# One core, attention with a SoLU layer: the order in which each engine's operations go out is taken from a table

## Chip, core and metric

The kernel runs on one NeuronCore of a Trainium2 chip. The metric is the time of the device in microseconds, the median of the runs shown. Engines are called by the profile's short names: PE (TensorE's matmuls), PEld (its weight loads), DVE (VectorE), ACT (ScalarE), POOL (GpSimd), SP (SyncE, which only issues DMAs here).

## What is computed

```python
def _attn_ref(q, k, v):             # 4 batches, 8 heads, 1152 positions, 64 wide
    q_pool = q.reshape(B, H, S // 2, 2, D).mean(axis=3)
    scores = scale * np.matmul(q_pool, k.transpose(0, 1, 3, 2))
    scores = scores - np.max(scores, axis=-1, keepdims=True)
    attn = np.exp(scores)
    attn = attn / (np.sum(attn, axis=-1, keepdims=True) + 1e-09)
    return np.matmul(attn, v)

def _moe_ref(x, w_in, w_out, g_ln):  # 2304 tokens, 512 -> 1024 -> 512
    h = x @ w_in
    e = np.exp(h - h.max(-1))
    solu = h * e / (e.sum(-1) + 1e-9)
    ln = (solu - mean) / np.sqrt(var + 1e-06) * g_ln
    return ln @ w_out
```

The output of the attention, heads side by side, is the x of the second part.

## The kernel before

The work is 32 heads (16 pairs), each with 9 blocks of 128 keys, and 18 tiles of 128 tokens. Nearly all products run as sums of f16 parts (a high and a low part of each operand), which is why every tensor is split before it is used.

For a pair P, `pair` (from line 614) loads K, Q and V, scales and splits them (tiles kn, qn on ACT and DVE), transposes the parts by DMA on SP (`k_turn`, `q_turn2`) and copies halves of them to other partitions (`k_stack`, `q_low`, `q_twice`, `q_half`). For a head g, `maxima` (from line 934) multiplies Q and K once to find the row maxima (PE at line 450 through the helper `mm`, DVE reductions mx at line 959), turns them into a row of shifts c5 and has SP write it into the operand q2 (`put`, lines 977 to 982). `scores` (from line 1092) then runs over the 9 key blocks j: two products of 288 columns each with the shift built in, Exp on ACT into e and eh (lines 1127 and 1133), the low part on POOL or DVE (line 1150), the products with V in PSUM bank 7 (`values`), and a division into the tile x.

When all 8 heads of a batch are done, `tokens` (from line 1286) takes their four or five tiles of tokens: split (xn), transposed by DMA (xt, line 1306), product with w_in into two banks, maxima, Exp, the product e (line 1338), the normalization (line 1375) with two small steps on POOL before it, the split into ln, its transpose (lt, ltt, line 1388), product with w_out, copy and store (lines 1441 and 1446). For the last batch nothing of attention is left beside this.

Nothing is issued straight away. Each step calls `Plan.add` (line 82) with an engine, a length in ns, a due time, a function that issues it, and the keys that it reads and writes. OFF (line 22) shifts the due time by key. `Plan.run` (line 110) plays a list scheduling: in simulated time each engine takes the ready operation with the earliest due time, with fixed costs for signals between engines, PSUM banks and rotating buffers. Where nothing is ready in the head it puts in a filler on PE (a transpose at line 1542). For SP the simulated end is that of the DMA:

```python
busy[e] = t + 640 * o.calls
dma = max(dma, t + 1200) + length
o.end = dma + KP.get("DL", 1000)
```

KP sets DL to 2000, and `TRD, TRC = KP["TR"]` are 300 and 2. At the end the functions are called in the order of their simulated starts (lines 284 to 286). That order is each engine's queue on the chip, and every engine works its queue off in order. Waits between engines are put in by the framework, from what is read and written.

Of the kernel before, what the change touches and what calls it, by code (L numbers as in the profile page):

```python
# [1573 lines left out]
```

## Time and profile before

| | us |
|---|---|
| median of 3 runs | 662.02 (661.11 to 669.67) |
| the profiled execution | 661.14 |
| its span | 659.4 |
| granted clock, mean | 0.986 |

A row of a timeline gives start, duration and what ran; in brackets stands how long the engine had been idle and what released it. Busy times of PE contain modelled ends, so neighbouring matmuls overlap in it. A granted clock of 1.00 is 2.4 GHz, of 0.50 it is 1.2 GHz.

### The profile page before, as it was taken

To read this page: it belongs to the slowest core of one execution; us is meant where nothing else is said; L and a number is where in the kernel's file an instruction comes from. 1 tells how busy PE (TensorE), PEld (TensorE's weight loads), DVE (VectorE), ACT (ScalarE), POOL (GpSimd) and SP (SyncE) were. 2 spreads that over 40 slices of the span, in tenths; PEclk is the share of its full clock that TensorE was granted. 3 is DMA by queue.
4 is the path that set the end of the run, shared out by engine and by line. 5 is a ranking of instruction groups with operands and counts; after the bars stand their busy time and mean duration, and the time that the engine had idled before them with its cause. 6 is when DMAs were issued, how large, how long until landed. Compare 5 with 4: busy or idle time off the path is not lost.

```text
span 659.4 us, 17549 instructions
## 1 busy us (share of the span) xinstructions
PE 607.0 (92%) x6821; PEld 422.1 (64%) x6821; DVE 493.6 (75%) x980; ACT 522.0 (79%) x1231; POOL 445.8 (68%) x376
## 2 busy tenths in 40 slices
PE   8986989899879899998999999998899999989996
PEld 7864877687556656675676666665566666654442
DVE  5997799889996977968697968696878875545450
ACT  4793778879898878988898989897889898864361
POOL 4692665559669877688878787867968689841140
PEclk9997999999999989999999999999999999999999
DMA  9786748694947667565758573939395642035444
GB/s 232 164 206 137 159 130 192 154 207 87 159 90 128 132 117 161 111 141 127 151 92 172 129 149 72 202 83 179 76 173 110 104 89 58 19 73 113 91 76 89
DMA packets 201903, 84.65 MB, mean 128 GB/s; under 512 B 189020, under 2 KB 189020, under 8 KB 201820
## 3 DMA queue, kind: packets, MB, share of 16 engines
q1 hardware_dynamic: 201820, 83.54, 60.9%
q8 instruction: 53, 0.87, 0.6%
q14 instruction: 30, 0.25, 0.1%
HBM read 36.70 MB, written 4.72 MB: 63 GB/s over the span
## 4 chain that ended last, share of the span: by engine, by line
PE 56%; DVE 17%; ACT 14%; DMA 5%; issue 4%; POOL 2%; SPq 1%; DVEq 0%; ACTq 0%; POOLq 0%
PE bank L450 53%; DVE mx L959 6%; ACT e L1127 3%; ACT eh L1127 3%; DMA xt<-xn 2%; PE bank L1542 2%; DVE kn L456 2%; DMA raw<-in_moe_w_out_dram 1%; DVE e L1375 1%; POOL eh L1150 1%; ACT e L1331 1%; DVE e L1338 1%; DVE qn L456 1%; ACT kn L715 1%; ACT vlo L847 1%
## 5 line engine op out<-in xcount | busy, mean ns | idle before, releaser
L1150 POOL TENSOR_TENSOR eh<-e,eh 128x576 f16<-128x576 f32 x255 | 337.3, 1333 | 115.7 <-ACT e L1127 35.4
L959 DVE TENSOR_REDUCE mx<-bank 128x2 f32<-128x768 f32 (+1 forms) x264 | 202.8, 785 | 48.2 <-PE bank L450 47.7
L1127 ACT ACTIVATE eh<-bank 128x288 f16<-128x288 f32 x384 | 151.5, 428 | 37.5 <-PE bank L450 36.0
L1127 ACT ACTIVATE e<-bank 128x288 f32<-128x288 f32 x426 | 166.5, 432 | 13.4 <-PE bank L450 7.8
L450 PE MATMUL bank<-q,w 128*128 128x288 f16 (+1 forms) x576 | 161.0, 291 | 8.7 <-ACT e L1127 3.5
L450 PE MATMUL bank<-q,w2h 65*128 65x288 f16 x540 | 150.2, 290 | 0.0
L450 PEld LDWEIGHTS <-eh 128*128 128x128 f16 x3855 | 138.2, 98 | 18.0 <-issue 2.3
L450 PE MATMUL bank<-vhi,eh 128*128 128x65 f16 x2570 | 143.1, 194 | 2.1 <-POOL eh L1150 1.1
L450 PE MATMUL bank<-vlo,eh 128*128 128x64 f16 x1285 | 133.4, 193 | 0.0
L450 PE MATMUL bank<-w,q 128*128 128x384 f16 (+1 forms) x390 | 101.7, 333 | 15.2 <-DVE mx L959 14.3
L450 PE MATMUL bank<-wb,lt 128*128 128x512 f16 x360 | 96.9, 381 | 7.3 <-DVE e L1338 5.7
L450 PE MATMUL bank<-wb,xt 128*128 128x512 f16 x360 | 98.0, 378 | 2.7 <-DMA xt<-xn 2.7
L450 PEld LDWEIGHTS <-w2h 65*128 65x128 f16 x540 | 53.1, 98 | 39.3 <-issue 12.0
L450 PEld LDWEIGHTS <-w 128*128 128x128 f16 x540 | 53.9, 100 | 30.3 <-issue 3.1
L450 PEld LDWEIGHTS <-lt 128*128 128x128 f16 x360 | 35.1, 98 | 34.2 <-issue 7.2
L450 PEld LDWEIGHTS <-q 128*128 128x128 f16 x360 | 33.5, 100 | 36.0 <-issue 21.0
L1133 ACT ACTIVATE eh<-bank 128x576 f32<-128x576 f32 (+1 forms) x75 | 46.8, 652 | 11.0 <-PE bank L450 10.7
L450 PEld LDWEIGHTS <-xt 128*128 128x128 f16 x360 | 34.1, 97 | 28.9 <-DMA xt<-xn 4.0
L1319 DVE TENSOR_REDUCE st<-bank 128x1 f32<-128x512 f32 x36 | 24.6, 684 | 28.7 <-PE bank L450 28.7
L450 PE MATMUL bank<-vx,eh 128*128 128x65 f32 x310 | 39.8, 276 | 0.0
L450 PEld LDWEIGHTS bank<-vx,eh 128*128 128x128 f32 x310 | 38.7, 196 | 0.9 <-issue 0.2
L1369 POOL TENSOR_SCALAR st<-st 128x1 f32<-128x1 f32 x18 | 5.1, 284 | 40.7 <-ACT ln L1360 40.0
(138 smaller groups left out, 833.5 us busy)
## 6 DMA issues: line engine op xcount, KB each, us to landing
kt<-in_k_dram SPq DMA_DIRECT2D x32, 288.0 KB
qt<-in_q_dram SPq DMA_DIRECT2D x16, 576.0 KB
vx<-in_v_dram SPq DMA_DIRECT2D x32, 288.0 KB
out_dram<-o SPq DMA_DIRECT2D x36, 128.0 KB
q<-q SPq DMA_DIRECT2D x30, 144.0 KB
w2h<-w SPq DMA_DIRECT2D x30, 144.0 KB
khi<-w SPq DMA_DIRECT2D x30, 144.0 KB
raw<-in_moe_w_in_dram SPq DMA_DIRECT2D x8, 511.6 KB
```

The costliest lines, as they stand in the source:

```text
L450: nc.tensor.matmul(out=o, lhsT=a, rhs=b, start=first, stop=last, skip_group_check=True)
L456: eng.scalar_tensor_tensor(out=o, in0=a, scalar=scale, in1=b, op0=ALU.mult, op1=ALU.subtract)
L715: nc.scalar.activation(out=o, in_=tl["kt", P], func=ACTF.Copy, scale=tl["qs", P][:, 2:3])
L847: nc.scalar.activation(out=new(("vlo", P), [128, 2, NJ, D], F16), in_=tl["vt", P], func=ACTF.Abs, accum_out=new(("am", P), [128, 1], F32),)
L959: nc.vector.tensor_reduce(out=flat(tl["mx", g])[:, i:i + n], in_=tl[place(i, n)], op=ALU.max, axis=AXX)
L1127: nc.scalar.activation(out=tl[name, (g, j)][:, f * HALF:(f + 1) * HALF], in_=tl[tn(j, f), (g, j, f)], func=ACTF.Exp, scale=esc,)
L1133: nc.scalar.activation(out=new((name, (g, j)), [128, SQ * 4 // mybir.dt.size(dtype)], dtype)[:, 0:SQ].rearrange("p (f i) -> p f i", f=2), ...
L1150: eng.tensor_tensor(out=e[:, o:o + c.stop - c.start], in0=e32[:, c], in1=e[:, c], op=ALU.subtract)
L1319: nc.vector.tensor_reduce(out=st(f), in_=tl[H_[f]], op=ALU.max, axis=AXX)
L1331: nc.scalar.activation(out=tl[E][:, f * 512:(f + 1) * 512], in_=tl[H_[f]], func=ACTF.Exp, bias=st(2), scale=xs[:, r, 3:4], accum_out=st(3 ...
L1338: nc.vector.scalar_tensor_tensor(out=tl[E][:, s], in0=tl[H_[f]], scalar=xs[:, r, 3:4], in1=tl[E][:, s], op0=ALU.mult, op1=ALU.mult, accum_ ...
L1542: plan.warm = lambda i: nc.tensor.transpose(bank[:, i, 0:128], ident, ident)
```

## The change

OFF gets new values for its 924 keys but the one for qn.5, which is new. A table SEQ is added: for each engine a string with one letter for each operation; the letter's code less 80 is a shift. The new method `line` sorts each engine's operations by their simulated start, as before, and then puts at place i the operation that stood at place i plus the shift. It also works out what each operation needs (its dependences, the users of the buffers and banks that it takes over, the makers of earlier buffers of the same tag), and calls the functions in an order that keeps these needs and each engine's own order. A new argument `late` adds to the simulated end of transposes by DMA. The engines, the buffers, the instructions and KP are the same.

```diff
--- before.py
+++ after.py
@@ -19,7 +19,8 @@
 AXX = mybir.AxisListType.X
 
...
-OFF = {'am.0': 15.58, 'am.1': 0.67, 'am.10': -8.76,
...
+OFF = {'am.0': 13.09, 'am.1': -0.54, 'am.10': -9.87,
...
+SEQ = {'PE': 'PPPPPPPPPPPPPPPPPPPPPPPPPQOPPPPPPPPPPPPPPPPPRPQRLOPPPPPPPPPPPPPPPPPPPPPPPPPPPPPPPPPPPPPPPPPPPPPPPPPPPPPPPPPPPPPPPPPPPPUOOSNOMPPQTPPRXNIPSOOOUIQ
...
 FIRST = KP.get("L0", 0.3)
 
 
@@ -79,9 +80,9 @@
                 yield from list(self.parts[k])
             yield k
 
-    def add(self, engine, length, at, fn, reads=(), writes=(), mark=None, kind="round", also=(), calls=1):
+    def add(self, engine, length, at, fn, reads=(), writes=(), mark=None, kind="round", also=(), calls=1, late=0):
         at += OFF.get(self.group((writes or reads)[0]), 0)
-        o = Op(n=len(self.ops), engine=engine, length=length, at=at, fn=fn, mark=mark, kind=kind, calls=calls)
+        o = Op(n=len(self.ops), engine=engine, length=length, at=at, fn=fn, mark=mark, kind=kind, calls=calls, late=late)
         deps = o.deps
         for k in self._keys(reads):
             if k in self.writers:
@@ -122,7 +123,7 @@
         for o in sorted(ops, key=lambda o: o.at):
             for b in o.new:
                 order[b[0]].append(b)
-        where, before = {}, {}
+        where, before, tags_of = {}, {}, defaultdict(list)
         ready = {e: [] for e in self.HOP}
         busy = dict.fromkeys(ready, 0)
         ranks = dict.fromkeys(ready, 0)
@@ -254,6 +255,7 @@
                     self.bank[b] = c
                 else:
                     turn[self.tags[b[0]][0]] += 1
+                    tags_of[self.tags[b[0]][0]].append(o)
                 head[b[0]] += 1
             for d in (*o.deps, *(x for b in o.uses for x in before.get(b, ()))):
                 known[e][d.engine] = max(known[e][d.engine], d.rank)
@@ -267,7 +269,7 @@
             if e == "SP":
                 busy[e] = t + 640 * o.calls
                 dma = max(dma, t + 1200) + length
-                o.end = dma + KP.get("DL", 1000)
+                o.end = dma + KP.get("DL", 1000) + o.late
             else:
                 busy[e] = o.end = t + length
             if o.mark is not None:
@@ -281,9 +283,51 @@
         if done < len(ops):
             raise ValueError([(o.n, o.engine, o.at, o.uses, o.left) for o in ops if o.start is None][:30])
         self.end = max(busy.values())
-        calls = [(o.start, o.n, o.fn) for o in ops] + [(t, -1, fn) for t, fn in extra]
-        for _, _, fn in sorted(calls, key=lambda x: x[:2]):
+        for fn in self.line(extra, where, tags_of):
             fn()
+
+    def line(self, extra, where, tags_of):
+        ops = self.ops
+        self.bufedges = defaultdict(set)
+        users, maker, tenant, need = defaultdict(list), {}, {}, {o: set(o.deps) for o in ops}
+        for o in ops:
+            for b in o.uses:
+                users[b].append(o)
+        for o in sorted(ops, key=lambda o: (o.start, o.n)):
+            for b in o.new:
+                maker[b] = o
+                for i in where[b]:
+                    if i in tenant:
+                        self.bufedges[o].update(users[tenant[i]])
+                    tenant[i] = b
+        for o in ops:
+            need[o].update(self.bufedges[o])
+            need[o].update(maker[b] for b in o.uses)
+            need[o].discard(o)
+        for made in tags_of.values():
+            for x, o in zip(made, made[1:]):
+                if x is not o:
+                    need[o].add(x)
+        self.need, self.items = need, {}
+        todo = {}
+        for e in self.HOP:
+            x = [(o.start, o.n, o.fn, o) for o in ops if o.engine == e]
+            if e == "PE":
+                x += [(t, -1, fn, None) for t, fn in extra]
+            x.sort(key=lambda x: x[:2])
+            self.items[e] = x
+            todo[e] = [x[i + ord(c) - 80] for i, c in enumerate(SEQ[e])] if SEQ else x
+            assert len({id(y) for y in todo[e]}) == len(x)
+        at, done, calls = dict.fromkeys(todo, 0), set(), []
+        while len(calls) < sum(len(x) for x in todo.values()):
+            heads = [(todo[e][at[e]][:2], e) for e in todo if at[e] < len(todo[e])]
+            heads = [(k, e) for k, e in heads if k[1] < 0 or need[todo[e][at[e]][3]] <= done]
+            _, e = min(heads)
+            _, _, fn, o = todo[e][at[e]]
+            at[e] += 1
+            done.add(o)
+            calls.append(fn)
+        return calls
 
 
 def MM(n, c=1):
@@ -755,7 +799,7 @@
             add("ACT", ACT(2 * SQ, 1, 1), at, k_hi, [KT, S_], [(*KN, 0)])
             add(*(("DVE", 2 * DVE(SQ) + 500) if P >= KP["KL"] else ("POOL", 2 * POOL(SQ))), at, k_lo, [KT, S_, (*KN, 0)], [(*KN, 1)])
             for h in range(2):
-                add("SP", TRD, at + KD * h + 0.5, lambda h=h: k_turn(h), [KN], [("w1", G + h, 0)], calls=TRC)
+                add("SP", TRD, at + KD * h + 0.5, lambda h=h: k_turn(h), [KN], [("w1", G + h, 0)], calls=TRC, late=1100)
             for h in range(2):
                 add("SP", DMA(64 * S * 2, 200), at + KD * h + 0.55, lambda h=h: k_stack(h), [("w1", G + h)], [("khi", P, h)])
 
@@ -824,7 +868,7 @@
             add("DVE", DVE(SQ) + 450, at, q_lo2, [*QT_, S_, (*QN, 0)], [(*QN, 1)])
             T, T1, T2 = ([(k, P, c, h) for h in range(2)] for k, c in (("q1", "T"), ("q1", "t"), ("q2", "t")))
             for h in range(2):
-                add("SP", TRD / 2, at + 0.5 + h / 10, lambda h=h: q_turn2(h), [QN], [T[h]], calls=TRC)
+                add("SP", TRD / 2, at + 0.5 + h / 10, lambda h=h: q_turn2(h), [QN], [T[h]], calls=TRC, late=1200)
             add("SP", DMA(64 * S * 2, 200), at + 0.8, q_low, T, T2)
             add("SP", DMA(64 * S * 2, 200), at + 0.9, q_twice, [*T, *T2], T1)
             add("SP", DMA(128 * 128, 200), at + 3, q_half, [("q1", P)], [("zq", P)], calls=2)
@@ -1391,7 +1435,7 @@
         SX = ("xs", r, 1)
         add("ACT", ACT(512, 1, 1), at, x_hi, [key, SX], [(*XN, 0)])
         add("DVE", DVE(512) + 400, at, x_lo, [key, (*XN, 0), SX], [(*XN, 1)])
-        add("SP", TRD, at + 0.2, x_turn, [XN], [XT], calls=TRC)
+        add("SP", TRD, at + 0.2, x_turn, [XN], [XT], calls=TRC, late=1100)
         for f in range(2):
             for c in range(6):
                 a = at + 1 + (6 * f + c) * step
@@ -1422,7 +1466,7 @@
             add("POOL", POOL(DF) + 80, a2, lambda: l_lo(nc.gpsimd), [E, (*LN, 0)], [(*LN, 1)])
         else:
             add("DVE", DVE(DF) + (700, 100)[tail], a2, lambda: l_lo(nc.vector), [E, (*LN, 0)], [(*LN, 1)])
-        add("SP", TRD * 2.5, a2 + 0.3, l_turn, [LN], [LT], calls=TRC)
+        add("SP", TRD, a2 + 0.3, l_turn, [LN], [LT], calls=TRC + 1, late=1100)
 
         def last(at):
             on = ("opn" if n % 2 else "opx") if tail else "ops"
```

## Rows read from the trace of the kernel before

**Rows 1.** Page, part 1: busy us, share of the span, instructions of each engine

```profile
PE 607.0 (92%) x6821; PEld 422.1 (64%) x6821; DVE 493.6 (75%) x980; ACT 522.0 (79%) x1231; POOL 445.8 (68%) x376
```

**Rows 2.** Busy time by stage: stretch, length, busy us (instructions) per engine, clock, DMA

```profile
0.00:60.00 60.00, 49.76 (x477) 42.42 (x478) 48.96 (x97) 40.53 (x65) 38.47 (x43) 0.98 0.82 194
60.00:240.00 180.00, 161.65 (x1855) 124.08 (x1855) 153.11 (x284) 147.36 (x302) 120.00 (x92) 0.96 0.69 143
240.00:580.00 340.00, 325.28 (x4087) 222.50 (x4085) 260.58 (x526) 298.50 (x798) 266.64 (x221) 1.00 0.58 118
580.00:659.40 79.40, 70.31 (x406) 33.07 (x404) 30.92 (x75) 35.60 (x68) 20.65 (x21) 0.99 0.47 91
```

**Rows 3.** Waits of PE: releaser, us in total, times, longest us

```profile
PE bank L450 <- DVE mx L959: 16.6, 23, 2.1
PE bank L450 <- DVE e L1338: 5.9, 6, 2.2
PE bank L450 <- DMA xt<-xn: 2.7, 4, 1.2
PE bank L450 <- DMA lt<-ln: 1.5, 1, 1.5
PE bank L450 <- DMA ltt<-ln: 1.1, 1, 1.1
```

**Rows 4.** Timeline of DVE, 194 to 232: start us, us, what

```profile
194.91 1.55 DVE L456 SCALAR_TENSOR_TENSOR kn<-kt,qs,kn 128x576 f16<-128x576 f32 x2
196.37 0.95 DVE L959 TENSOR_REDUCE mx<-bank 128x2 f32<-128x768 f32 x1
...
229.03 1.95 DVE L456 SCALAR_TENSOR_TENSOR kn<-kt,qs,kn 128x576 f16<-128x576 f32 x2 [0.54 <-ACT kn L715]
230.99 0.75 DVE L1338 SCALAR_TENSOR_TENSOR e<-bank,xs,e 128x512 f32<-128x512 f32 x1
```

**Rows 5.** Timeline of PE at the same two places: [idle before <-releaser]

```profile
197.38 0.60 PE L450 MATMUL bank<-w,q 128*128 128x384 f16 x2 [2.12 <-DVE mx L959]
...
231.80 1.44 PE L450 MATMUL bank<-wb,lt 128*128 128x512 f16 x3 [2.25 <-DVE e L1338]
```

**Rows 6.** Busy time in stretches of 2.5 us behind the two lulls

```profile
197.50:200.00 2.50, 2.50 (x16) 1.61 (x15) 1.71 (x2) 2.35 (x6) 2.32 (x4) 0.52 0.63 147
200.00:202.50 2.50, 2.50 (x39) 2.18 (x37) 1.89 (x2) 1.60 (x6) 2.42 (x4) 0.79 1.38 147
...
232.50:235.00 2.50, 2.50 (x9) 1.21 (x8) 1.81 (x7) 0.18 (x1) 1.38 (x1) 0.50 0.76 176
```

**Rows 7.** Line 1542, the fillers: duration min/median/max, first and last start us

```profile
L1542 PE MATMUL bank<-ident x89: 270/273/477, 1.6 to 21.6; 128*128 128x128 f32 x89
```

**Rows 8.** Chain that ended last, one of its transposes: start us, us, what

```profile
413.66 4.47 DMA xt<-xn
```

**Rows 9.** Timeline of PE in the tail

```profile
589.40 5.34 PE L450 MATMUL bank<-wb,lt 128*128 128x512 f16 x24 [1.87 <-DVE e L1338]
594.58 5.34 PE L450 MATMUL bank<-wb,xtt 128*128 128x512 f16 x24
601.44 3.63 PE L450 MATMUL bank<-wb,lt 128*128 128x512 f16 x16 [1.52 <-DMA lt<-ln]
...
649.49 5.35 PE L450 MATMUL bank<-wb,ltt 128*128 128x512 f16 x24 [1.15 <-DMA ltt<-ln]
```

**Rows 10.** Line 1375, the normalization: duration ns min/median/max

```profile
L1375 DVE TENSOR_SCALAR e<-e,st x15: 811/1631/1874, 200.2 to 634.5; 128x1024 f32<-128x1024 f32 x15
L1375 DVE TENSOR_SCALAR et<-et,st x3: 811/812/814, 606.0 to 640.1; 128x1024 f32<-128x1024 f32 x3
```

**Rows 11.** Waits of SP's queue, and PE's wait for the copy of q

```profile
SPq L980 <- DVE c L971: 48.9, 12, 10.9
...
PE bank L450 <- DMA q<-q: 0.4, 1, 0.4
```

More of the change, by code (lines that the diff above doesn't have):

```diff
@@ new lines @@
+SEQ = {'PE': 'PPPPPPPPPPPPPPPPPPPPPPPPPQOPPPPPPPPPPPPPPPPPRPQRLOPPPPPPPPPPPPPPPPPPPPPPPPPPPPPPPPPPPPPPPPPPPPPPPPPPPPPPPPPPPPPPPPPPPPUOOSNOMPPQTPPRXNIPSOOOUIQNTUPRLURRFJQLSPPQQKPPPPPRRNNPPQQNPPPPPPPPPROOPPPPPPQOPPPPPPPPPPPPPPPPPPPPPPPPPPPPPPPPRRNQQVKUPMMNNPPPTQQMMPPPQOROOPROOPPPPPPPPPPPPPPPQQNPPPROOPTQVVLLOLRRLLROORRRMQLRRRTLPKYNOPPPLQNQMPPQOPPPPPRRNQMPPPQOPPPQQQQLPTOSSMSQSSISHTLNRTVLRRJLQQJQQNPQQNPROOROOROOPPROOPPPPPPPPPPVOQQMMOPUOOOOOPPSOOOPPPQRNQNPROOPPSOOQQMPPUPNOSNNOPPQOPPPPPPPPPPPPPPPQQNPPROOQQNPROQQMTOOOOPROOPPPROQQMPPQOPPQQNTTUPMQLIQOROOPROOROOROOPRRNNPPPSPNQNPPPPPPPPPQOTROSNPJPPQOSOORSOLUQMNOOPPRRRNLRROSQRRIQKRPRRLNYPNQRPLLPNROOQOPROOPPSSOOQKSORRMRROQQHPPPPROOPRZOPPQJNTOMRMMPPPRYSMMSPLXKOLPNPNQQMPQOQQNPPPTOPPMPPPPQOPPPPPPPPPPPPPPPQQNQOROOPPPPPQOPPPPQOPPPRSNNOPQOPPPPPQOPPPPPROQNPQRNOSQNQMPQTPMPNQOPPPPPPPPPPQQRPQQQQQQQQQQBPPPPPPPPQOPPPPPPPPPPROOQQQMPVPPMTNNNRTQLPLUPTMOMNSVTMPTKKSQRRRKGRPQMPQOQQNSOORNSNOOROUNOOOOQOPPPQOPROOQOPWOPPMOOOQQNPPPPQQNQOPPPQQNPPPPPPPSQSMMOPPPSOOOPPPRUOPPPJPPPQORROQLPPQOPPROOPQOPPSSNXQWKQNPMSNUOCPPMPPQQNPPPPSOOOPPPPPPPPPPQOPPPPPPPPPRRNQMPQOVVNQULLLVLPTVSMMQGKUOPSORNJPPROOPSOOOPSOOQRMQNPQOPPROOQSTMSNOQQSHOSPPQKPQOPPPPPPRTNPPLPPQOPPPQOQQNSUOOPKQNSORVQQKKRORRKRPQQJPPPPPROOPTPNPSSLNNPSSNOSLRNNPPPPPRROQLQOSO]NPMOOOPPMPPMRNOQSNORRMNSSSSMMRTHNOOPPSUNQNRORPHSOROTPQJNTOPNOQOPPQQQRLQNQRSZZMYMHMMYLYKQQIJHUROTJSIWLPSOJUMPPKQUMPNPUMPNOOPPTOPNRPQLQOQ[YPNOJYNLNLMQLNOTQQMQTPJOOPQXQQQQQIJOPPPPPPRPNPPPQOPPPQQNRPRRSKMOPWQQNPKPUPTOOIRPQQQIPPPRRNSQLQMVQQRLOSTRTRFSUWTVFOQDRVTUEOORKWAPPUSTTLMRRTDPVQDMQOSQUNRORFQRPQIQRSMXRNQUMUNFSSU\\RHSTTHSVRAWSEGHPLOQYUOLPNOKRRNQKRTRMORRJQQRTVPHRNRNSSFRTQKKOPPQOPPPQOPPPPZO[NPP]KNOOHPJPLPPPTWOOOQVNOCORNNSSSMNRRJNPPPPPPPPPPPPPPUUUMMMMQLPPPPPPPPPPPPPPPPPPPPPROQQQLUOTNSMRLQ]J\\\\\\_KKY\\I[HHH[[VPYOSSV?W>VRRTTVSS6666PPPPPPUUUMTLLLQQQQHPPPPPPPPPPPPPPPQQNPPPPPPPPPP', 'ACT': 'PPPPPQOPPPPPPPPQOPPPPPPPPPPPQOUPPMRNRRLNPQQQQQQQIPPPPPQOSOOOQOPUOPNPNPPPROOPQOPQOPQQQQQRJQQRPKPQOPPPQRNOPQOPQQQQLUOOOPNPPSQNQQQQQRPQRRUNRORRM=PPPPPQOPROOPPQOPPPSOPNTQOPLPPQQQRPRPRPQQQDPPPPPQOPQOPQQNPRSNPMPPQOPROOPQRNQNPQOQQNQQRMSNPNPPQOQOPQQQRPQJQOQOQOQOPPPPPPPPPPPPPQOPROOQQQTPPPQHPQOPRRNNUOPPMOSTNOPLQQNPQOPPPQOQOQOPPQOPPQOPRSNNQNQOSQNQMPPPPPQOPSOROQQKPPPROQYMOPNOPNPNRPQMPQOQOPQOQOQQNPPQQQMPPPPPPPPPPPPPPPPPPROQNPUOPPMOPPQOPPQOPQOPPPPPPROOQRNOQQRMORPQQRPJQOPPPPQOPPPPQOPPPPQOQOPPPUOOPNSQMRPQKPQOPROOQOPRPNQQNQOQOPPSPPQQQRPQQQEQOQOPQQNQORPNPPPPPPPPQOPQOPQOPPPQOPPPPPUOOOPNPQOPPPPPRPNPPPQOPPPPQOPPPPQOPPPPPPQOPPQRNQNPPPQOQOROQNPPQOPPQORSOPLPPQOPPPPPPRPQMPQQNROSSTLMMOPPPSPNRNOPQRROQRJORORNQNPQOPPPQOPPQOQOPPPPPPPQOPROOPPROOPPPPQOPRPRPLQRPQQQRRRSMSQRRAQQQQGQQNPQOQOROOPTOOPNROOPPQOPPPPPPPPPRO[PMOPPMOQNNOTOPNOURRNNKQOQOQORPQQRPQQRPQQQCQRNOPPQOQQNQOPPQOPPROWNOOQNNOROQNPPQOPPPPPPPPPPPPROQNPPPPXOOPNPNVOMQNPMROOPPPQOPQOQOPPQQNPPROQNPPPPPPPPPPPPPPPPQOQORPNQOQOPQRPMQQQQQQQQQRPQRRBQSPPQQHPPRPNPPPPPPQORPNPWOPNQOMOPQRNOPQOPQQQQLQOPPPPPPPROQNPQRNOPQQNQOQQNQQNPPPPPQQNPPPPPPPPPPQOROQNPTOPPMPPQOPPQQNPPPPQOPPQOPPQOPPQORPQMPVOOPNOOQOPPPQQNPQQRMQNPPPPPRRNQRPQQQQQFPQOPPP', 'DVE': 'PPPPPPPPPPPPPPPPPQQQTPQOSQOQRPCPQOSOPNQOPROOPRPNQOPQOSOPQMQOPPPTVTMNSSJKRPRIQQQRSQNQQRRRNSASNNRNQQQQQQQRGRRRNQQQHPPPPPPPPPPPPPPPPPPPQRNOPPQRNOQOUOPNOOPPPPPPQOROOQOPSQNNPPQOQOPPPQOlPQMQOLOOPNOOPNOOOUOMNNNPMQRNQKPQOPPPPPQRPQQQJPPPPPPPPPPPPPPPPQQNPPTTNORRRRRRRFRRRRRRAJPPPPQOPPPPPPPPPPPPQRNOQOPQOPQQNQQNQQQQRPRPHYOOOOPNOOOQSNTOQRRRIKQOPPQOPPTQOTOSOOSTOUPRSARSHPQQQGQRNQNPPQOPPPPPSOPNPQOQQSPPQRRRGMPPPQQQQQQQQQQQQQQQRPQQQQQ:QOPPPRSTNLPSSKSMWOPJPPMOPQQQRPQQQQRPQRTVNO?NOOPRROMPPPPQVQMNTNSNSNPQHPPPPPPPPPPPQUPPPROQQGQORPQQLPPPPPSOTOMOXQMNOWNPQLQKQQQQQQQQRPQQRP@QOQOSPNQQMQRNOPQQQQQQSTVGNQUM`HPLQOKOaNNNOMNPNPKQNQQLSUNOQRNFRPQRPKQQQMQQNPPROQQQLPPPPWXVMMNLMSQSJSQHZLOOOOOOUNNNOOPPPPPPPSQNSMOQSTUKaLPKLOORRRRRRRRTUEUDNSPR@KRTOMORROSQSNRRNQQQQTPQOT<PUMQOTKTTLSMKMVVWMTWTJJJURRYMSPROBSSNXMWWNPMMORLQQQQ.QRPQLQQQUPUJPMMQNPPPPQRRRLMSPRRLTPPPQRROQRRRNRRR=QQRJOPQQQQLQRSOPKQQNPPQOPSOOOPQQRPLPPPPPQOPP', 'POOL': 'TRSSLLRPQQQQQQQQQQQQQQQQQQ8PPPPPQOPPPPPPPPPPPPQOPQOQQQQQKQQQMQOPPPPQQQQLPPPQOPPPPPPQOPPPPPPPPPPPQOPPPPPPPPPPPPQQNPPQOPQOPPPPPPPPPPPPPPPPPPPPPPPPPPPPPPPPPPPPPPPPPPQOPPPPPPPPPPPPPPPPPPPPPPPPPPPPPQOPPPPPPPPPPPPPPQQNQQQQLPPPPPPPPPPPQQQQLPPPPQOPPPPPPPPPQOQOPPPPPPPPPPPPPPPPPPPPPPPPPPPPWOOOOOOOPPPPPPPPPPPPPPPPPPPPPPPPPROOPPPPPPPPPPPPPPPPPRRRRRKQJPPPPPPPPPPPPPPPPPPPPP', 'SP': 'PPPPPQQNPQQQQQKROOSSVSLRKKRRRRTTTOENQFSPNOPPROOQOPPPRPQQRRRIRLRNRPMPPRRSQMSSOOGQRRSLPLQQNPQOQSPPQKQQQQLPP[PNOOOOOPNORPQLRPNQSPMOQOPPQRNQNPSTNOSUKRPRSQRRVQSQDUQLSXNTPSKUSQSSSSURTTTTN)R^VQOPPRR6RROSST0TLQSXLRVO=KPNSQRRMRREQTQYJOLORPSMSNPQRRRTTQWJSVKSP:SQRXQQQWCVVWLM>XIPQWQQNRPSQRRR>QRTRPMRROQSSTO0RRNQRROTQOVTVQO=LSQNRPUPQQ@QSSSTMSFOJPUPPQLSMROQLSQRMMPPQO'}
```

2 lines of the change are left out of this document (1 added, 1 removed).

## Prediction

> **What bounds the kernel now.** I read four views. The busy times of the engines first: TensorE's matmuls fill 92% of the span, ScalarE 79%, VectorE 75% [rows 1]. So the most that an order alone can give back is what TensorE waits: 659.40 - 607.00 = 52.4 us. Then the same times by stage [rows 2]: the head (0 to 60) leaves TensorE idle for 60.00 - 49.76 = 10.2 us, the first batch of heads (60 to 240) for 18.4, the long middle (240 to 580) for 14.7, the tail for 9.1. In the middle ScalarE is busy for 298.5 of 340 us (88%), so there a second engine is close behind; from 60 to 240 VectorE is (153.1 of 180, 85%).
>
> Third, who TensorE waits for [rows 3]. The maxima's reductions on VectorE (tile mx, line 959) hold it longest, 16.6 us in 23 waits, because they free the PSUM banks into which the next maxima go; the product e on VectorE (line 1338) comes next with 5.9 us in 6 waits; transposes that land late (xt, lt, ltt) make 2.7 + 1.5 + 1.1 = 5.3 us. Fourth, the order of time around the worst lulls. At 194.91 VectorE starts the two kn subtractions (1.55 us); only then, at 196.37, comes the reduction mx, and TensorE stands for 2.12 us until it is done [rows 4, 5]. At 229.03 the two kn again (1.95 us) go ahead of e, and TensorE stands for 2.25 us [rows 4, 5]. Behind each such wait stands all of TensorE's queue, also matmuls that are ready. Each lull also costs clock: in the stretches behind them the granted clock is 0.52, 0.79 and 0.50, while TensorE is busy all of the time [rows 6]. 0.50 is the lower of its two levels, 1.2 of 2.4 GHz.
>
> **The change part by part.** (1) No instruction is added or removed. Counting the add calls in the loops gives 1,722 TensorE operations; with the 89 warm-up fillers [rows 7] that is 1,811, exactly the length of TensorE's string in the table. So the fillers stay, and with them the head up to about 21.6 us. Cost: nothing.
>
> (2) The order moves much. In the strings 1,162 of TensorE's 1,811 entries, 718 of ScalarE's 1,160, 660 of VectorE's 885, 104 of GpSimd's 362 and 306 of SP's 354 are not zero; at the least 560, 328, 279, 30 and 146 single operations must have been moved. The 924 due-time shifts in OFF, from which the list scheduling starts, are new too (median step 3.0 us). The strings alone don't name operations, so what they gain has to be bounded stage by stage.
>
> (3) The planner's landing times of transposes grow. For xt it planned 1,200 + 300 + 2,000 = 3,500 ns from issue, now 4,600 with late=1100; for lt 3,950, now 4,600, and three instead of two issue slots of 640 ns on SP. The trace has 4.47 us for xt [rows 8]. So a plan that counted on xt 1.0 us too early becomes right. It moves no work; its gain is a part of the 5.3 us above and is counted in the stages below.
>
> Now the stages; the bounds of each are nothing and the whole of its idle time.
>
> The two lulls: if the short operation goes ahead of kn, mx starts 196.37 - 194.91 = 1.46 us earlier, and e 230.99 - 229.03 = 1.96 us [rows 4]. The clock behind them costs 0.48 x 2.5 + 0.21 x 2.5 + 0.50 x 2.5 = 3.0 us [rows 6]. Together 6.4. What is late next is kn, by one mx (0.95) or one e (0.75), and behind it the transposes of K for the next pair on SP. I take half, 3.2 us, since nothing shows that the new order takes these places apart and makes no others.
>
> The other idle time: mx and e make 16.6 + 5.9 = 22.5 us of the 52.4 - 4.6 = 47.8 us that lie ahead of the last matmul's end (649.49 + 5.35 = 654.84) [rows 3, 9], about half. These an exchange of neighbours can shorten; but the reduction itself, 0.95 us of a wait of some 2.1, has to run all the same. Half of a half is a quarter. Head, without the 1.6 us before the first filler [rows 7]: (10.2 - 1.6) / 4 = 2.2. From 60 to 240 without the two lulls: (18.4 - 2.12 - 2.25) / 4 = 3.5. Middle: 14.7 / 4 = 3.7.
>
> Tail: three stalls, 1.87 + 1.52 + 1.15 = 4.5 us, on e and on transposes of LN [rows 9]; the 4.6 us behind the last matmul (copy and store) no order takes away. From 601.44 on, TensorE runs without a gap but for the last stall, so there is little else to put in: a third, 1.5 us.
>
> New waits: the planner counts with one length for an operation, and lengths here depend on what runs beside it. The normalization at line 1375 takes 0.81 us at best, 1.63 in the median and 1.87 at worst; in the tail, where GpSimd is busy for a quarter of the time (20.65 of 79.4 us), the three of tile et are all at 0.81 [rows 2, 10]. If the new order put all 15 at the longest against their median, that would be 15 x (1.87 - 1.63) = 3.6 us of VectorE's time; if it put all at the shortest it would give 12.3 back. Other operations do the same, and TensorE's new waits come on top. I put 3.0 us against the change, between nothing and all that it gains.
>
> The Trainium skill has a rule that speaks against a search on fixed lengths: "SBUF — State Buffer" (Who interferes with whom) says that VectorE and GpSimd share a port pair, that whoever issues first takes it for its whole instruction, and that issue order decides who blocks. The spread of line 1375 [rows 10] fits it, but no row here shows the port. By the rule the third term could be of either sign and as large as the 12.3 us.
>
> Sum: 3.2 + 2.2 + 3.5 + 3.7 + 1.5 - 3.0 = 11.1 us. The profiled execution took 661.14 us (span 659.40), so 650.0. The median of the runs shown is 662.02, 0.9 above it; I predict **651 us** as a median, 1.7% below.
>
> **The rivals.** *A, the forecast:* a quarter of the waits goes; 651, own range 644 to 657.
>
> *B, the stalls only change places:* what TensorE no longer waits for VectorE it waits for ScalarE, at 88% in the middle [rows 2]. For it: the waits are spread over 23 places of some 0.7 us each [rows 3]; against it: ScalarE still has 41.5 us of idle time there. Nothing but the 1 to 2 us of late transposes is won: 660.
>
> *C, a search this fine fills most holes:* half of the idle time from 60 to 580, (18.4 + 14.7) / 2 = 16.5, the 3.0 of clock, 2.2 in the head, 1.5 in the tail, no new waits: 661.14 - 23.2 + 0.9 = 639. For it: over 1,300 moved operations and landing times that now agree with the trace. Against it: an order by a planner transfers only as far as its lengths hold [rows 10]. In this connection the Trainium skill ("Perfetto Trace Analysis", Identifying the Most-Contended Engine) takes matmul busy time for a bad measure of TensorE's headroom and weight-load busy time for a good one: 64% here. By it there is more to win than 52 us, which speaks for C. The trace agrees in part: a block of 24 matmuls shows 5.34 us, and the next block starts 594.58 - 589.40 = 5.18 us after it [rows 9], so a modelled end hides up to 0.16 us of waiting at each gap.
>
> *D, slower, a blocked SP queue:* all loads, transposes, copies and stores go out on SP in order. Its write of the shift row (line 980) waited 48.9 us for c5 in 12 waits, 4.1 each, and all DMAs behind it wait along [rows 11]; now nothing of TensorE's time shows it (0.4 us on q) [rows 11]. With 306 of 354 entries shifted, by up to 39 places, a transpose or a load may come to stand behind such a wait. For the 15 pairs after the first, a quarter of 4.1 us exposed in each is 15 us, and two more stretches at the lower clock 2: 661 + 17 = 678. It decides from (675.3 - 661.1) / 15 = 0.95 us a pair on. Against it: the planner's plan contains the SP queue.
>
> That the order isn't changed at all is excluded by the strings.
>
> **How the numbers follow.** Chances: A 0.50, B 0.20, C 0.20, D 0.10. 2% of 662.02 is 13.2 us, about what a measurement of this kernel can tell from no change: faster below 648.8, slower above 675.3. Faster: C, and two fifths of A (its part below 648.8): 0.20 + 0.20 = 0.40. Slower: most of D, 0.08. Within: the rest, 0.52. The range of 8 in 10 takes in A and B and most of C: 638 to 664; A's own is 644 to 657.
>
> **What would show it.** Right: TensorE's idle time below 45 us, mx waits below 13 us, e waits below 4; granted clock from 60 to 240 above 0.97 (0.96 before [rows 2]); no wait of TensorE over 1 us on xt. The same busy times for TensorE within 2%, and 89 fillers. B: TensorE's waits for mx fall and those for ScalarE's e and eh grow by as much. C: idle below 32 us. D: TensorE's waits for DMA above 10 us, with waits of SP on c5 ahead of them. Wrong altogether it would be if VectorE's or GpSimd's busy sum moved by more than 15 us at equal work: then lengths, not order, would decide.

## The result, and the profile after

The changed kernel takes 643.64 us as a median of 4 runs (643.11 to 647.8), the kernel before 661.94 beside it: a ratio of 0.9712, 95% interval 0.9629 to 0.9795. It is 2.9% faster. The forecast was 651, so the direction and the range held, but the gain is 18 us where the sum had 11.1. The profiled execution took 643.11 us, with a span of 641.3. Each ratio in what follows is to the kernel before as it was timed beside that kernel (medians of 661.94 to 667.52 us), and leaves out slow executions with a lower clock.

The page of the changed kernel, part 1 (busy us, share of the span, instructions), answers to [rows 1]:

```profile
PE 605.3 (94%) x6821; PEld 423.8 (66%) x6821; DVE 501.3 (78%) x980; ACT 520.8 (81%) x1231; POOL 449.8 (70%) x376
```

The same 6,821 instructions, nearly the same busy time. TensorE's idle time fell from 52.4 to 641.3 - 605.3 = 36.0 us. VectorE is busy for 7.7 us longer, and TensorE waits less for it all the same (mx and e in the rows below).

Stretches of equal time hold unequal work now, so the stages of [rows 2] are cut anew, at the divisions (tile x) of head 8, head 11 and head 31, which both kernels execute once each (that a head is reached means in what follows that its division starts). First the kernel before, then the changed one; columns as in [rows 2]:

```profile
0.00:185.24 185.24, 163.21 (x1724) 132.72 (x1725) 157.41 (x300) 141.14 (x244) 115.15 (x101) 0.97 0.75 166
185.24:242.81 57.57, 50.81 (x625) 35.08 (x623) 47.47 (x84) 48.78 (x130) 45.67 (x37) 0.94 0.63 123
242.81:588.05 345.24, 330.20 (x4189) 226.54 (x4188) 259.76 (x528) 301.50 (x806) 269.40 (x223) 1.00 0.57 117
588.05:659.40 71.35, 62.78 (x288) 27.73 (x287) 28.93 (x70) 30.58 (x54) 15.53 (x17) 0.99 0.47 91
```

```profile
0.00:185.98 185.98, 166.46 (x1727) 135.49 (x1728) 157.36 (x300) 141.44 (x246) 114.39 (x101) 0.95 0.70 165
185.98:237.48 51.50, 48.46 (x624) 33.58 (x622) 44.89 (x83) 48.92 (x130) 44.49 (x37) 1.00 0.61 120
237.48:572.67 335.19, 327.84 (x4187) 226.69 (x4184) 269.39 (x526) 301.19 (x807) 275.37 (x223) 1.00 0.62 122
572.67:641.30 68.63, 62.51 (x288) 28.01 (x288) 29.68 (x73) 29.29 (x50) 15.54 (x17) 1.00 0.52 100
```

Up to head 8 nothing is won: 185.24 against 185.98 us. Heads 9 to 11, where the two lulls were, take 6.1 us less and the granted clock is 1.00 there in place of 0.94. Heads 12 to 31 take 10.0 us less, more than all the rest, with the clock at 1.00 in both. The tail takes 2.7 less. Together 18.1.

TensorE's waits of the changed kernel (releaser, us in total, times, longest), which answer to [rows 3]:

```profile
PE bank L494 <- DVE mx L1003: 12.2, 20, 1.6
PE bank L494 <- ACT wb L628: 2.4, 4, 0.8
PE bank L494 <- DMA lt<-ln: 2.2, 1, 2.2
...
PE bank L494 <- ACT e L1177: 1.5, 3, 0.9
```

The waits for the product e (5.9 us before) and for xt (2.7) are gone; mx fell from 16.6 to 12.2; no other releaser has taken their place by more than 2.4 us.

Where the first stretch loses is seen in TensorE's timeline of the changed kernel, in those rows that start after a wait (in brackets: idle before, releaser), and in the granted clock (the number after the five engines) of stretches of 2.5 us:

```profile
58.43 0.48 PE L494 MATMUL bank<-w,q 128*128 128x384 f16 x2 [0.89 <-DVE mx L1003]
...
59.96 0.48 PE L494 MATMUL bank<-w,q 128*128 128x384 f16 x2 [0.59 <-DVE mx L1003]
61.49 0.80 PE L494 MATMUL bank<-w,q 128*128 128x384 f16 x2 [1.05 <-DVE mx L1003]
...
120.93 0.38 PE L494 MATMUL bank<-wb,id 128*128 128x512 f16 x1 [0.76 <-ACT wb L628]
122.22 0.28 PE L1012 MATMUL bank<-ident,m 128*5 128x128 f32 x1 [0.92 <-DVE xs L1320]
```

```profile
59.50:62.00 2.50, 0.99 (x4) 0.45 (x4) 2.24 (x5) 1.93 (x4) 1.27 (x1) 0.89 0.69 126
...
64.50:67.00 2.50, 2.50 (x12) 1.46 (x11) 2.19 (x4) 1.49 (x3) 0.00 (x0) 0.50 1.06 177
...
125.50:128.00 2.50, 2.50 (x25) 2.33 (x22) 1.38 (x3) 0.01 (x1) 1.33 (x2) 0.50 0.83 256
```

There are waits of up to 1.05 us in a row near 60 and near 121 us, and behind each group the clock is at its lower level, 0.50, also in stretches in which TensorE is busy all of the time.

### The profile page after: what moved, and what is told of

Read it like the earlier page. It is cut to its first block, busy times and chain, and to the rows that moved or that the text cites. A ratio compares the mean times of both kernels' runs of the same rounds, so it can differ in the third digit from the quotient of the medians.

```text
span 641.3 us, 17577 instructions
## 1 busy us (share of the span) xinstructions
PE 605.3 (94%) x6821; PEld 423.8 (66%) x6821; DVE 501.3 (78%) x980; ACT 520.8 (81%) x1231; POOL 449.8 (70%) x376
## 4 chain that ended last, share of the span: by engine, by line
PE 59%; DVE 20%; ACT 10%; issue 4%; POOL 4%; DMA 2%; SPq 1%; POOLq 0%; ACTq 0%; DVEq 0%
PE bank L494 56%; DVE mx L1003 7%; ACT e L1171 3%; DVE kn L500 3%; ACT eh L1171 3%; POOL eh L1194 2%; PE bank L1586 2%; DVE vlo L940 1%; DVE e L1419 1%; DVE qn L500 1%; DMA lt<-ln 1%; ACT eh L1177 1%; ACT e L1375 1%; DVE xn L500 1%; DVE wb L500 1%
## 5 line engine op out<-in xcount | busy, mean ns | idle before, releaser
L1171 ACT ACTIVATE e<-bank 128x288 f32<-128x288 f32 x426 | 169.2, 422 | 20.3 <-PE bank L494 10.9
L1171 ACT ACTIVATE eh<-bank 128x288 f16<-128x288 f32 x384 | 154.5, 424 | 11.6 <-PE bank L494 9.9
L494 PEld LDWEIGHTS <-eh 128*128 128x128 f16 x3855 | 134.7, 98 | 13.0 <-issue 2.7
L494 PE MATMUL bank<-vhi,eh 128*128 128x65 f16 x2570 | 138.9, 194 | 1.0 <-DVE vs L908 0.5
L494 PE MATMUL bank<-vlo,eh 128*128 128x64 f16 x1285 | 130.6, 193 | 0.0
L494 PE MATMUL bank<-w,q 128*128 128x384 f16 (+1 forms) x390 | 109.5, 337 | 12.5 <-DVE mx L1003 11.8
L494 PE MATMUL bank<-wb,lt 128*128 128x512 f16 x360 | 94.3, 378 | 2.2 <-DMA lt<-ln 2.2
L494 PEld LDWEIGHTS <-w2h 65*128 65x128 f16 x540 | 53.0, 98 | 41.6 <-issue 11.1
L1177 ACT ACTIVATE eh<-bank 128x576 f32<-128x576 f32 (+1 forms) x75 | 47.7, 657 | 19.6 <-PE bank L494 19.5
L494 PEld LDWEIGHTS <-xt 128*128 128x128 f16 x360 | 34.7, 97 | 26.3 <-issue 1.3
L1177 ACT ACTIVATE e<-bank 128x576 f32<-128x576 f32 x44 | 28.8, 657 | 7.4 <-PE bank L494 7.4
L565 POOL TENSOR_TENSOR up<-up,un 128x512 f32<-128x512 f32 x16 | 20.7, 1296 | 19.1 <-ACT un L558 10.0
```

Source lines behind the costliest of these rows:

```text
L494: nc.tensor.matmul(out=o, lhsT=a, rhs=b, start=first, stop=last, skip_group_check=True)
L565: nc.gpsimd.tensor_tensor(out=up, in0=up, in1=tl["un", n].bitcast(F32), op=ALU.subtract)
L1171: nc.scalar.activation(out=tl[name, (g, j)][:, f * HALF:(f + 1) * HALF], in_=tl[tn(j, f), (g, j, f)], func=ACTF.Exp, scale=esc,)
L1177: nc.scalar.activation(out=new((name, (g, j)), [128, SQ * 4 // mybir.dt.size(dtype)], dtype)[:, 0:SQ].rearrange("p (f i) -> p f i", f=2), ...
```

## Experiments

The shares of the change first, then the steps of the prediction, then what is still to be had. All kernels but the last group do exactly the work of the reference with the same instructions.

**The table or the due times?** Two kernels. *no_table* is the changed kernel with an empty table, so new OFF and `late` under the list scheduling:

```diff
-SEQ = {'PE': 'PPPPPPPPPPPPPPPPPPPPPPPPPQOPPPP...
+SEQ = {}
```

> The changed kernel with an empty table: each engine goes by the list scheduling's order again, from the new due times and with the later landing of transposes. Theory (the single moves of the table carry the gain): between 655 and 668 us, near the kernel before, and TensorE's waits for mx back above 14 us. Rival (new due times and landing times carry it, the table adds little): 643 to 648 us.

Measured: 661.94 us, ratio 0.9957 [0.9921, 0.9993]. The table carries nearly all of the gain: 2.4 of 2.9 per cent. The strings permute the new list, so the table on the old due times can't be run, and the two shares are not independent. The stages of no_table, at the same divisions, show that the due times move much all the same; then its waits of TensorE:

```profile
0.00:191.63 191.63, 167.27 (x1724) 134.65 (x1725) 158.51 (x300) 141.79 (x244) 116.61 (x100) 0.95 0.72 160
191.63:245.61 53.98, 48.13 (x620) 33.01 (x619) 47.04 (x82) 47.92 (x130) 45.19 (x36) 1.00 0.63 123
245.61:589.00 343.39, 331.67 (x4193) 226.87 (x4190) 262.15 (x531) 301.48 (x807) 270.99 (x224) 1.00 0.59 118
```

```profile
PE bank L494 <- DVE mx L1003: 11.9, 13, 3.4
PE bank L494 <- ACT eh L1171: 5.0, 13, 1.1
PE bank L494 <- ACT e L1171: 4.6, 12, 1.1
PE bank L494 <- ACT e L1177: 4.1, 7, 0.9
```

Head 8 comes 6.4 us later than in the kernel before, heads 9 to 11 take 3.6 us less, with the clock at 1.00 already, heads 12 to 31 1.9 less. The time was as expected, the wait for mx was not: it stays at 11.9 us, where more than 14 had been expected. What comes back without the table are the waits for ScalarE's e and eh: 15.8 us (eh of line 1177, 2.1, included), against 7.9 in the kernel before and 4.8 in the changed one. So the new due times took 4.7 us of the waits for mx away and brought 7.9 us of others for ScalarE, and the table took away those.

*late_only* is the kernel before with the later landing times (`late=`) alone and, for lt, the third issue slot, as in the diff above.

> The kernel before with nothing but the later landing of transposes in the plan (and three issue slots for lt). Theory: the late transposes cost the kernel before some 5 us of TensorE's time at most, so 656 to 664 us, with TensorE's waits on xt near nothing. Rival (the plan's wrong landing times were the main loss): 650 us or less. A third case: the due times were fitted to the old landing times, so that the order gets worse, above 665 us.

Measured: 701.59 us, ratio 1.0554 [1.0471, 1.0637]. Its waits of TensorE:

```profile
PE bank L450 <- DVE mx L959: 26.3, 32, 1.8
PE bank L450 <- ACT e L1127: 11.7, 24, 1.2
```

No wait for a transpose stands at the top: mx and e do. A wait for xt (2.7 us before) isn't among TensorE's waits any more, so the later landing does what it is there for. But the order gets worse elsewhere, mx from 16.6 to 26.3 us, e of line 1127 from 3.5 to 11.7, and the kernel takes 5.5% longer, until new due times (no_table) bring it back. That the old due times suited the short landing times alone would explain it; no run shows that this is the reason.

**Early or late part?** The table for operations whose list start lies ahead of 186 us, or behind it, the list order for the others:

```diff
...
+            y = [x[i + ord(c) - 80] for i, c in enumerate(SEQ[e])]
+            a, b = (y, x) if EARLY else (x, y)
+            todo[e] = [z for z in a if z[0] < CUT] + [z for z in b if z[0] >= CUT]
```

> The changed kernel with the table applied only to operations that the list scheduling starts before 186 us (about the first eight heads); behind that the list's own order. Theory: heads 0 to 8 end no earlier with the table (185.2 us before, 186.0 after), so nearly nothing is won against the empty table, at most 4 us. Rival (the table works everywhere alike): 186 of 640 us, so about 0.3 of what the whole table wins over the empty one.

> The changed kernel with the table applied only to operations that the list scheduling starts from 186 us on. Theory: nearly the whole gain, within 4 us of the changed kernel (643 to 648 us). Rival: 0.7 of what the whole table wins over the empty one.

Measured: 658.24 us, 0.9874 [0.9776, 0.9972] for the early part, 649.56 us, 0.9772 [0.97, 0.9845] for the late one. From no_table's 661.94 these are 3.7 and 12.4 us; their sum is 16.1 of the 18.3 between no_table and the changed kernel. By the ratios the sum is 0.8 + 1.9 = 2.7 points, where the whole table has 2.4, so within the intervals the two parts make up the whole. In the traces the early part reaches head 8 at 185.66 us, no_table at 191.63: 6.0 us, of which 4.3 are given back by head 31 (401.7 against 397.4 us from head 8 on). The late part goes from head 8 to head 31 in 387.1 us, the whole table in 386.7.

**The two lulls.** *swap_two* is the kernel before with the two exchanges on VectorE that my first term counted on, *swap_first* only the first of them (place 285):

```diff
+            for i in (285, 328) if e == 'DVE' else ():
+                x[i], x[i + 1] = x[i + 1], x[i]
```

> The kernel before with two exchanges on VectorE: the kn subtractions of two pairs go behind the next operation, the reduction mx at 196 us and the product e at 231 us. Theory (the step of the two lulls): mx starts 1.46 us earlier and e 1.96 us, TensorE's waits of 2.12 and 2.25 us shrink to under 1 us, and the clock behind them stays up: 3 to 6 us less than the kernel before. Rival (kn is late next and its transposes hold the next pair back by as much): within 1 us of the kernel before.

> The kernel before, with one exchange on VectorE only: at 196 us the reduction mx goes out ahead of the second kn. All work is the same. Theory 1 (the half of my first step that held in the run with both exchanges holds alone): the wait of 2.12 us becomes about 0.8, the clock stays at 1.00 behind it, and the time falls by the 0.4 to 2 us that head 9 gave there: 660 to 661.5, where 0.8 to 1.3 of waiting and 1.7 of clock would allow 2.5 to 3.0. Theory 2 (stalls only change places): what is won at 197 is given back before 240, the time is 662 within 0.5. Told apart by the division of head 9 and of head 11.

Measured: swap_two 667.25 us, ratio 1.0044 [1.0013, 1.0074]: 0.4% longer, a small loss where 3 to 6 us of gain were expected. First TensorE's row at the first lull in swap_two, then VectorE's at the second, then a stretch behind the first with its clock:

```profile
197.33 0.49 PE L496 MATMUL bank<-w,q 128*128 128x384 f16 x2 [0.80 <-DVE mx L1005]
```

```profile
232.34 0.75 DVE L1384 SCALAR_TENSOR_TENSOR e<-bank,xs,e 128x512 f32<-128x512 f32 x1 [2.49 <-ACT e L1377]
```

```profile
197.50:200.00 2.50, 2.28 (x40) 1.84 (x39) 2.50 (x3) 2.50 (x7) 2.50 (x2) 1.00 0.48 118
```

The mx half holds: the wait falls from 2.12 to 0.80 us and the clock stays at 1.00 where it was 0.52 [rows 6]; but head 9 then takes 19.19 us in place of 19.61, so 0.4 us is left of it, and head 10 gives it back (15.6 us in place of 15.1). The e half falls: e can't go ahead at 229, because ScalarE's Exp that it multiplies with isn't there; VectorE stood for 2.49 us with kn behind it, and head 11 took 24.7 us in place of 22.9. The trace of the kernel before had the row that tells this:

```profile
230.02 0.84 ACT L1331 ACTIVATE e<-bank,st,xs 128x512 f32<-128x512 f32 x1
```

That Exp ends at 230.86, and VectorE's e starts at 230.99 [rows 4]: 0.13 us was to be had there, not 1.96. swap_first alone gives 663.5 us, ratio 0.9988 [0.9949, 1.0027]: not to be told from nothing. Its head 9 again takes 19.19 us and head 10 15.5.

**Whose order matters?** Three kernels in which one engine, or all but one, leave the table and take, among the operations whose needs have been issued, the one with the earliest start in the list scheduling (that is not the list's own order, so they show what an order can cost and not what the table gained over the list):

```diff
...
+LOOSE = ('SP',)
...
+            for e in LOOSE:
+                x, i = todo[e], at[e]
+                j = next((j for j in range(i, len(x)) if x[j][1] < 0 or need[x[j][3]] <= done), i)
+                x.insert(i, x.pop(j)) if i < len(x) else None
```

> The changed kernel with the table's order on all engines but TensorE; there the ready operation with the earliest start in the list scheduling goes out next. Theory (VectorE's and ScalarE's order lets the short operations go first, TensorE's own order matters most since it is the fullest engine and all that stands behind a wait stands still): half or more of the table's 18 us is lost, 652 to 662 us. Rival (TensorE's order follows from the others): 643 to 650 us.

> The kernel after with TensorE's string alone: each other engine takes, among the operations whose needs have been issued, the one that starts earliest in the list scheduling. All work is the same. Theory 1 (TensorE's own order carries the gain, the others follow): within 6 us of the kernel after, 643 to 650. Theory 2 (the strings only work together, since TensorE's order was found against the fixed order of the others): TensorE's waits for VectorE's mx and ScalarE's e grow by over 15 us, 660 and above.

> The kernel after without SP's string: SP issues, among the DMAs whose needs have been issued, the one that starts earliest in the list scheduling; the other four engines keep the table. All work is the same. Theory 1 (SP's order has slack, and 306 shifted entries of 354 only follow the other engines): within 2 us of the kernel after, 642 to 646. Theory 2 (the mechanism of my case D: a transpose or load that comes to stand behind the write of a shift row is exposed): TensorE's waits for DMAs grow by 5 us or more, 649 and above.

Measured: without TensorE's string 747.28 us, 1.1256 [1.1192, 1.132]; with TensorE's string alone 836.03, 1.2591 [1.2509, 1.2673]; without SP's 679.14, 1.0207 [1.0134, 1.028]. The first is far above both cases expected (at most 662). Without its own string TensorE waits 28.5 us for mx and 11.4 and 8.2 us for ScalarE's e and eh. So, with this order in place of the strings left out, TensorE's string alone doesn't carry the gain, and the other four without it don't either. No run shows what one string gains over the list's own order. The run without SP's string shows a blocked SP queue, the ground of my slower case, D. Its waits of TensorE, then of SP's queue:

```profile
PE bank L499 <- DMA q<-c: 19.0, 6, 7.5
...
PE bank L499 <- DMA q<-q: 8.2, 3, 4.6
```

```profile
SPq L1029 <- DVE c L1020: 59.8, 8, 12.7
```

SP waits for c (and 48.5 us for qn) in single stretches of up to 12.7 us, with other DMAs behind them, and TensorE waits 27.2 us for writes of the shift row and copies of q. D had a transpose or a load standing behind the write of the row; here it is mostly the write itself (19.0 us) that comes late. One went out at 256.17 us behind a transpose of ln that had waited 3.2 us for its operand, and TensorE stood for 2.80 us. In the changed kernel SP waits for c even longer than before in sum (37.9 us in 6 and 23.0 in 8 waits, against 48.9 [rows 11]), and TensorE waits for no such DMA at all. So the length of SP's waits does not decide; I take it that what stands behind them does.

**What the clock costs.** The changed kernel with fillers (transposes of the identity, 0.27 us each, as in the head) in TensorE's queue, in a PSUM bank that is free there: 32 around 57 to 63 us and 14 around 121 us (*fill_both*), or only the 14 (*fill_second*). In the table of places a pair gives the bank and the number of fillers. Nothing of the computation is changed; 46 or 14 instructions are added.

```diff
+FILL, MOVE = {200: (2, 6), 203: (2, 7), 205: (2, 5), 207: (2, 8), 209: (2, 6), 369: (2, 6), 370: (2, 8)}, ()
...
+            for i in sorted(FILL, reverse=True) if e == "PE" else ():
+                b, n = FILL[i]
...
+                todo[e][i:i] = [(todo[e][i][0], -1, lambda b=b: self.warm(b), None) for _ in range(n)]
```

> The changed kernel with 46 more warm-up fillers on TensorE, in the waits for mx at 57 to 63 us and in the waits at 120 to 122 us (into a PSUM bank that is free there). Theory (the new order gains nothing in the first eight heads since the lower clock behind these two lulls takes it back: 10 us at 0.50 from 122.5 to 133 and 5 us from 64 to 69 with TensorE busy, up to 7 us): clock at 1.00 there and 637 to 641 us. Rival (the lost matmul time lies beside work of ScalarE and VectorE that sets the pace): clock at 1.00 and 642 to 645 us. Slower: fillers hold back the operations that wait there, above 645 us.

> As fill_both, with only the 14 fillers at 120 to 122 us. Theory: clock at 1.00 from 122 to 133 us and two thirds of what fill_both wins, 639 to 642 us. Rival: no change, 642 to 645 us.

Measured: fill_both 637.72 us (637.13 to 639.28, 5 runs), ratio 0.9605 [0.9561, 0.965]; fill_second 641.22 (637.99 to 644.69, 6 runs), 0.9654 [0.961, 0.9697], not to be told from the changed kernel by their intervals. The clock of fill_both in one of the stretches shown above:

```profile
64.50:67.00 2.50, 2.50 (x23) 1.99 (x21) 2.40 (x4) 1.59 (x3) 0.00 (x0) 1.00 0.84 137
```

Its mean over the execution is 1.000 (0.987 in the changed kernel), and head 8 is reached at 182.32 us in place of 185.98. This is the fastest kernel of the study, some 6 us below the changed one; the two kernels were timed beside different runs of the kernel before, and their ratios' intervals overlap a little (0.9629 to 0.965), though every run of fill_both is shorter than every run of the changed kernel.

*fill_before* does the same with the kernel before: 37 fillers at its own waits from 54 to 62 us.

> The kernel before, with 37 fillers (transposes of the identity into PSUM bank 0, whose scores have been read) put into TensorE's queue ahead of five products for the maxima, where it waits from 54 to 62 us. The work of the reference is untouched. Theory 1 (the lower clock behind short waits costs by itself, whatever the order): the granted clock from 57 to 68 us goes from 0.50 to 1.00, the 4.5 us of full work that run at half speed from 63.0 to 67.5 become 2.3, and the time falls by 2 to 3.5 us: 658.5 to 660. Theory 2 (the waits there are for VectorE, whose 1.9 us a step set the pace, and what comes behind waits again): the clock rises but the time stays within 1 us.

Measured: 664.46 us, ratio 0.9982 [0.9945, 1.0019]: no difference that can be told. Its clock, then the ScalarE row behind which it lost again:

```profile
62.00:64.50 2.50, 2.18 (x30) 1.88 (x28) 2.50 (x4) 1.87 (x4) 0.00 (x0) 1.00 0.31 68
...
110.00:112.50 2.50, 2.50 (x13) 2.06 (x13) 0.52 (x2) 1.02 (x2) 2.50 (x2) 0.50 0.29 118
```

```profile
105.06 1.16 ACT L898 ACTIVATE vlo<-vx 128x1152 f16<-128x1152 f32 x1 [3.47 <-DMA vx<-in_v_dram]
```

The clock around 60 us is 1.00 in place of 0.50, and head 3 is reached at 97.99 us in place of 101.28. But then the load of V isn't there: ScalarE waits 3.47 us for it (1.52 in the kernel before), TensorE behind it, a new lull at 104 to 106 us brings the clock down again, and head 4 comes at 118.11 in place of 116.38. So the fillers give what they should at their place, and in the old order the next late thing, a load, takes it. That this is the reason in every execution isn't shown; one was profiled.

## Why the prediction was right, and where its steps failed

**The sum.** By the same cuts: up to head 11 I had 3.2 + 2.2 + 3.5 = 8.9 us and 5.3 came (242.81 to 237.48); heads 12 to 31, 3.7 against 10.0; the tail, 1.5 against 2.7; the new waits, -3.0, have no counterpart. 11.1 against 18.1: the middle and the new waits together are 9.4 too low, the tail 1.2 too low, the front 3.6 too high. That the total came within 7 us is in part luck: the errors have both signs.

**The middle is the mis-sized term.** I argued that mx and e make half of the waits, that an exchange of neighbours can make each about half as long because the reduction itself has to run, and so came to a quarter. TensorE's waits in heads 12 to 31, of the kernel before (242.81 to 588.05 us) and then of the changed one (237.48 to 572.67):

```profile
PE bank L450 <- DVE mx L959: 4.2, 8, 1.1
PE bank L450 <- ACT e L1127: 3.2, 9, 0.6
PE bank L450 <- DMA xt<-xn: 2.5, 3, 1.2
PE bank L450 <- DVE e L1338: 1.6, 3, 1.1
PE bank L450 <- DVE xs L1276: 0.9, 1, 0.9
```

```profile
PE bank L494 <- DVE mx L1003: 3.5, 6, 1.1
PE bank L494 <- ACT e L1171: 0.8, 3, 0.4
PE bank L494 <- ACT eh L1171: 0.7, 3, 0.3
```

mx, from which I had worked out the quarter, hardly moved: 4.2 to 3.5. What went are the other waits, nearly whole: ACT's e 3.2 to 0.8, xt, the product e and xs from 2.5 + 1.6 + 0.9 to nothing. That is 7.4 us; the idle time fell from 345.24 - 330.20 = 15.04 to 335.19 - 327.84 = 7.35, so by 7.7. It went in two steps: in no_table it is 343.39 - 331.67 = 11.7 us, with these waits:

```profile
PE bank L494 <- ACT eh L1171: 3.6, 9, 1.1
PE bank L494 <- ACT e L1171: 1.8, 7, 0.5
PE bank L494 <- DVE e L1382: 1.8, 2, 1.4
...
PE bank L494 <- DVE mx L1003: 0.8, 2, 0.5
```

So xs and xt (0.3 us left) go without the table, and late_only, with the later landing alone, has no wait for xt at all; what is left of ScalarE's e and eh and of the product e goes with the table. Even mx falls to 0.8 us without the table, and comes back to 3.5 with it.

How a wait can go whole is seen at the first of the three waits for xt. TensorE's busy time and, in brackets, its matmuls up to the issue of the transpose on SP, then up to the product that reads it; first the kernel before, then the changed one:

```profile
0.00:413.66 413.66, 378.76 (x4441) 0.98 0.67 145
0.00:418.18 418.18, 382.10 (x4471) 0.98 0.68 145
```

```profile
0.00:403.85 403.85, 376.82 (x4404) 0.98 0.68 147
0.00:408.41 408.41, 381.38 (x4470) 0.98 0.68 146
```

The product has kept its place in TensorE's order, 4,471 and 4,470 matmuls in; the transpose goes out 37 matmuls earlier, and the 4.5 us from its issue to the product are filled. At the second wait it is the same (the product at 4,823 and 4,827, the transpose at 4,808 and 4,747); at the third the matmuls in between are fewer but longer, and the transpose goes out 5.62 us ahead of its product in place of 4.73. So more of TensorE's work lies between the issue and the product, at the first 66 matmuls where there were 30, and the wait goes whole. My bound, that the producer's own length stays in each wait, was the step that failed; it held for none of the waits that went. Which moves took away those for ScalarE's e and for the product e isn't shown.

The other 2.4 us are busy time (330.20 to 327.84): the same matmuls overlap more closely; by which neighbours, I didn't try. The 10 us are well clear of what executions of one order differ by: fill_before, with the old order there, takes 348.4 us for these heads, fill_both, with the new one, 334.4.

**The two lulls:** the 6.1 us of heads 9 to 11 are nearly the 6.4 that I had as the bound and halved. The place was right (idle 6.76 to 3.04 us, clock 0.94 to 1.00), the way wasn't: swap_two shows that of my two exchanges one gives 0.4 us and the other loses. My 1.96 us for e came from VectorE's timeline alone; I hadn't looked whether e's other operand, from ScalarE, was there at 229, and it came at 230.86. The new order got there by other moves, and 3.6 of the 6.1 us by the new due times alone (no_table).

**Head and first batch up to 185 us:** nothing of the gain counted there came. Idle time fell (22.0 to 19.5 us), but busy time rose by 3.3 at a clock of 0.95 for 0.97. fill_both shows what became of it: with the clock held up, 3.7 us come out up to head 8. I had counted the clock's price only behind the two lulls that were to go, and not that the new order leaves others (and makes the one at 121 us).

**Landing times:** that they move no work of themselves was right, and the wait for xt goes with them alone (late_only). That a plan with true times becomes right as a whole was not: late_only is 5.5% slower. One wait for lt stayed, and grew from 1.5 to 2.2 us.

**New waits:** of VectorE's lengths no price is to be seen. Its sum rose (kn 27.2 to 30.2 us, the low part of V 11.5 to 15.7, the normalization 20.7 to 18.0), by 7.7 us in all, within the 15 I had set, and TensorE waits less for it. New waits did come, for ScalarE's wb (0.2 to 2.4 us) and of a filler in the head for mx (2.0); they lie in the stages above, so the 3.0 us can't be told apart from the other terms. The row of the normalization, answering to [rows 10]:

```profile
L1419 DVE TENSOR_SCALAR e<-e,st x15: 792/1144/1766, 204.7 to 616.4; 128x1024 f32<-128x1024 f32 x15
```

Its median fell from 1631 to 1144 ns at the same span of lengths. The Trainium skill's rule of the shared port ("SBUF — State Buffer", Who interferes with whom), by which issue order decides who blocks, agrees with lengths that change with the order alone; that it is the port no run here shows.

**The rivals.** For the whole change B is excluded: mx fell by 4.4 us, and ScalarE's e and eh didn't grow (no row of theirs over 1.5). But its sign is just what no_table shows: mx down by 4.7 us, e and eh up by 7.9, and a time within 0.4% of the kernel before. B holds for the due times, and the table is what goes beyond it. C asked for idle below 32 us; it is 36.0, between A's 45 and that, as the time is between 651 and 639. C was right that much of it can be won, and with the fillers the kernel does reach it (637.72); but that is clock, not a better order. D didn't happen, and free_sp shows that it was no empty threat: another order of SP costs 5% against the changed kernel (1.0207 for 0.9712), with the writes of the shift row late themselves rather than holding up the rest.

**Signs I had set:** idle below 45, mx below 13, e below 4, no wait over 1 us on xt, TensorE's busy time within 2%, 89 fillers: all as said. The clock from 60 to 240 above 0.97: wrong, it is 0.95.

## What to carry to other kernels

When an order changes, size each wait by asking how much of the waiting engine's other work can lie between the producer's start and the operation that needs it. Where that covers the time of the producer, the whole wait goes: here for a transpose, with 66 matmuls in between where there were 30. When waits for one engine shrink, look whether those for another have grown by as much, before it is called a gain. Before an exchange is priced, look at every operand of the operation that is to go first, on every engine. And look at the granted clock behind the waits that stay: here 46 fillers, put where the bottleneck engine stood idle, were worth as much as a third of the whole change, and in the old order, where a load was late right behind, 37 were worth nothing.
